# An attention and expert kernel: the router's early pass at another place, and another opening

## The chip, the cores and the metric

One of the eight cores of a Trainium2 chip runs the kernel. The metric is the device time of one execution in microseconds; several executions are timed, and the median is taken. The engines have two names each in what follows: TensorE is PE (its weight loads PEld), VectorE DVE, ScalarE ACT, GpSimd POOL, SyncE SP.

## The reference

Attention over 8 batches of 12 heads, 448 positions, 64 numbers per head; then its output is the input of an expert layer with 8 experts.

```python
q_n, k_n = rmsnorm(q, g_q), rmsnorm(k, g_k)          # x / sqrt(mean(x*x) + 1e-6) * g
scores = q_n @ k_n.T / 8;  attn = softmax(scores);  x = attn @ v
logits = x @ w_gate                                   # 3584 tokens, 8 experts
# all (token, expert) pairs in order of falling logit: a token goes to the first expert
# that still has fewer than 448 tokens
out[tokens of e] = relu(x[tokens of e] @ w1[e]) @ w2[e]
```

## The kernel before

The 96 heads are worked on in 24 groups of four (two pairs of heads). A group's q and k are loaded as rows (three quarters of each head's positions on 128 partitions, 192 numbers each, by `_load`; the last 64 positions of each head, the tails, by `_tail` or `_tails`), squared on ScalarE (L308), summed on VectorE (L320), turned into an inverse root by a logarithm and an exponential on ScalarE (L326, L328) and a correction (L337 to L339), scaled (L353, L381), split into two f16 parts (L386, L391, L420, L425), transposed, and used in three kinds of products on TensorE: a first pass that only finds row maxima (`max_scores`, L539 and L542; VectorE takes the maxima, L553), the scores (L572; ScalarE's exponential, L583), and the products with v (L607), whose results VectorE divides and ScalarE and VectorE split into two f16 parts (`x_norm` L642 to L646, `x_hi` L657 and L658, `x_lo` L663 and L664). The transposed scores come out with the keys on the partitions, so nothing is transposed there. Each pair of heads takes one bank of PSUM for its products with v, out of a ring of two banks called po. Every finished pair's x is transposed on TensorE in part (`x_here`, L681) into the same bank before the bank is given on.

Groups 0 and 1 are worked on in halves, one per pair of heads, so that TensorE gets work early. Until then dummy matmuls with the identity (`busy`, L216) keep it active; `BUSY` has their numbers. `spread` puts the product of the two norm scales g_q and g_k on all partitions by a matmul with a row of ones (L206); `spread_out` copies it to gg, by which GpSimd multiplies q (L381).

After attention comes the router. It finds for each token its best expert and an integer key, and compares the keys with thresholds; then it searches counts. `early` (L1296) does this first step for the 21 of 28 columns of tokens that belong to batches 0 to 5, as soon as their logits are there: 12 VectorE instructions (L1253 to L1263 and the compare of 128x672, L1293). The same step for the last 7 columns follows at the end of attention (the late pass). Then the experts run.

The order of all this is written out by hand, as a table: `plan` adds each step as a task with its engine or queue, what it needs and what it makes, and the table `ORDER` names the tasks two characters at a time in the order in which they are issued, so each engine's instructions stand in that order in its own line. "Yr" is the task of `early`. A step may stand anywhere in the table behind what it needs. Loads go to the queue of SyncE ("S") or ScalarE ("A"); a load that is the ninth, tenth and so on waits until the load eight before it has landed, as its semaphore is used again.

## Time and profile before

| what | |
|---|---|
| median of 3 runs | 909.04 us (906.68 to 910.67) |
| the profiled execution, its own time | 905.66 us |
| its span, first to last instruction | 903.9 us |
| TensorE busy | 860.5 us (95%) |
| VectorE, ScalarE, GpSimd busy | 642.7, 467.7, 390.4 us |
| mean granted TensorE clock | 0.982 |

Times in the profile count from the start of the span. Busy shares are averages over the whole; what a change at one place is worth is read from the rows of that place. In a timeline a row is one instruction or a run of equal ones; "[4.56 <-DVE xm L664]" says that the engine was idle for 4.56 us before it, and what ended that. A queue's rows (SPq, ACTq) are the issues of loads, not their landing. PEclk is the granted clock of TensorE as a share of 2.4 GHz; 0.5 is 1.2 GHz.

### The profile page before, as it was taken

What the parts mean: (1) busy time and instruction counts of PE and PEld (TensorE: products, weight loads), DVE (VectorE), ACT (ScalarE), POOL (GpSimd) and SP (SyncE); (2) the same over time, 40 slices, a digit from 0 to 9 for tenths busy, and PEclk for the clock granted to TensorE, in tenths of its full rate; (3) what the DMA queues carried; (4) which work ended last, traced back from release to release, by engine and by line L of the source; (5) the groups of instructions that cost most, each with busy time, mean ns of one, the idle gap of its engine ahead of it and who ended that gap; (6) DMA issues with size and microseconds to landing.
All of it is one profiled execution on the core that took longest, in us unless ns stands there. A gap on an engine that the chain in (4) does not pass through costs nothing.

```text
span 903.9 us, 27548 instructions
## 1 busy us (share of the span) xinstructions
PE 860.5 (95%) x11763; PEld 558.4 (62%) x11765; DVE 642.7 (71%) x1539; ACT 467.7 (52%) x739; POOL 390.4 (43%) x400
## 2 busy tenths in 40 slices
PE   5999999999999997995999999999999999999996
PEld 2467677777777776784556555565555655556553
DVE  6999999889988988737887776866768675143100
ACT  5987887788777874650434333323333333242110
POOL 7899998889989886001103021101111120200001
PEclk9999999999999998995999999999999999999998
DMA  7669998999999895413747195685929397591001
GB/s 188 154 153 204 189 206 175 230 186 226 161 211 199 202 171 135 90 28 137 269 146 255 38 293 171 206 231 164 253 92 279 140 251 219 170 244 43 27 18 44
DMA packets 253019, 153.64 MB, mean 170 GB/s; under 512 B 178654, under 2 KB 240094, under 8 KB 251872
## 3 DMA queue, kind: packets, MB, share of 16 engines
q1 hardware_dynamic: 247388, 129.39, 60.8%
q0 software_dynamic: 4704, 22.03, 7.4%
q8 instruction: 92, 1.51, 0.7%
q10 hardware_dynamic: 804, 0.46, 0.2%
q14 instruction: 31, 0.25, 0.1%
HBM read 94.43 MB, written 22.02 MB: 129 GB/s over the span
## 4 chain that ended last, share of the span: by engine, by line
PE 59%; issue 18%; DVE 11%; DMA 4%; POOL 3%; ACT 3%; SPq 1%; POOLq 0%; DVEq 0%; ACTq 0%
PE ph L1807 15%; PE py L1824 13%; PE po L607 12%; PE psc L572 10%; DVE mx L553 3%; PE py L1833 2%; PE pm L542 2%; DMA q<-qs 1%; DMA qkraw<-in_q_dram 1%; ACT e L583 1%; POOL out_dram L1843 1%; PE psc L542 1%; POOL rows L1740 1%; PE rp L1453 1%; DVE st L337 1%
## 5 line engine op out<-in xcount | busy, mean ns | idle before, releaser
L1807 PE MATMUL ph<-xt,w1h 128*128 128x448 f16 (+2 forms) x804 | 209.4, 344 | 0.0
L607 PEld LDWEIGHTS po<-v,e 128*64 128x64 f32 (+1 forms) x5376 | 173.5, 137 | 41.8 <-issue 21.8
L607 PE MATMUL po<-v,e 128*64 128x65 f32 (+1 forms) x5376 | 187.4, 224 | 2.3 <-DVE xt L374 1.1
L583 ACT ACTIVATE e<-psc 128x896 f32<-128x896 f32 x168 | 151.2, 915 | 48.5 <-PE psc L572 40.9
L572 PE MATMUL psc<-q,k 128*64 128x448 f16 x1344 | 156.1, 355 | 1.3 <-DVE mx L553 0.9
L1843 POOL DMA_INDIRECT out_dram<-y,idx x32 | 34.4, 1076 | 279.9 <-ACT y L1826 245.6
L1807 PE MATMUL ph<-xt,w1l 128*128 128x448 f16 (+2 forms) x402 | 135.1, 344 | 0.0
L1824 PE MATMUL py<-w2l,hh 128*128 128x384 f16 x384 | 125.0, 326 | 0.0
L1824 PE MATMUL py<-w2h,hl 128*128 128x384 f16 x384 | 125.0, 326 | 0.0
L1824 PE MATMUL py<-w2h,hh 128*128 128x384 f16 x384 | 125.0, 326 | 0.0
L1807 PEld LDWEIGHTS <-w1h 128*128 128x128 f16 x804 | 74.0, 97 | 63.8 <-issue 2.3
L553 DVE TENSOR_REDUCE mx<-pm 128x2 f32<-128x896 f32 x96 | 104.0, 1084 | 10.4 <-PE pm L542 7.8
L1795 ACT ACTIVATE hh<-ph 128x448 f16<-128x448 f32 x64 | 34.8, 544 | 144.3 <-PE ph L1807 139.6
L1824 PEld LDWEIGHTS <-hh 128*128 128x128 f16 x768 | 73.3, 97 | 46.4
L572 PEld LDWEIGHTS <-k 128*64 128x64 f16 x1344 | 75.2, 110 | 30.1 <-issue 5.7
L1826 ACT ACTIVATE y<-py 128x384 f32<-128x384 f32 x48 | 23.6, 491 | 132.6 <-PE py L1824 104.1
L1740 POOL DMA_INDIRECT rows<-xd,idx x32 | 31.9, 997 | 130.1 <-DVE idx L1634 43.2
L1797 DVE SCALAR_TENSOR_TENSOR hl<-ph,hh 128x448 f16<-128x448 f32 x64 | 39.2, 619 | 60.4 <-ACT hh L1795 60.2
L553 DVE TENSOR_REDUCE mx<-psc 128x2 f32<-128x896 f32 (+1 forms) x74 | 77.8, 1056 | 5.2 <-PE psc L542 4.5
L1727 DVE SCALAR_TENSOR_TENSOR w2l<-stage,w2h 128x768 f16<-128x768 f32 x64 | 60.2, 951 | 22.2 <-ACT w2h L1723 22.1
L1727 DVE SCALAR_TENSOR_TENSOR w1l<-stage,w1h 128x768 f16<-128x768 f32 x64 | 59.4, 950 | 3.3 <-ACT w1h L1723 3.3
L1723 ACT ACTIVATE w1h<-stage 128x1536 f16<-128x1536 f32 x32 | 47.2, 1476 | 21.5 <-DMA stage<-in_moe_w_dram 21.5
(294 smaller groups left out, 1434.3 us busy)
## 6 DMA issues: line engine op xcount, KB each, us to landing
stage<-in_moe_w_dram SPq DMA_DIRECT2D x64, 768.0 KB
vraw<-in_v_dram SPq DMA_DIRECT2D x24, 384.0 KB
xd<-xb SPq DMA_DIRECT2D x8, 1152.0 KB
qkraw<-in_q_dram SPq DMA_DIRECT2D x23, 384.0 KB
qkraw<-in_k_dram SPq DMA_DIRECT2D x23, 384.0 KB
vraw<-in_v_dram SPq DMA_DIRECT2D x24, 64.0 KB
xd<-xm SPq DMA_DIRECT2D x16, 96.0 KB
qkraw<-in_k_dram SPq DMA_DIRECT2D x22, 64.0 KB
```

The lines of the kernel that those rows point to most:

```text
L553: self.nc.vector.tensor_reduce(m, p[:, :k, :448], axis=AX.X, op=OP.max)
L572: nc.tensor.matmul(p[64 * h:64 * h + 64, i, :448], kt[:, a, n + 64 * h:n + 64 * h + 64], qt[:, a, 448 * s:448 * s + 448], start=st, stop=n ...
L583: self.nc.scalar.activation(e, p[:, :, :448], AF.Exp, scale=scale)
L607: self.nc.tensor.matmul(self.po(pair)[64 * n:64 * n + 64, w], self.T["e", d][r, i, q:q + 64], self.v1[g % 2][r, self.slot(a, u, s)], start ...
L1723: self.nc.scalar.activation(h, v, AF.Copy, scale=self.WS)
L1727: self.later(0.93, lambda w=w: self.nc.vector.scalar_tensor_tensor(l[:, w], v[:, w], self.WS, h[:, w], op0=OP.mult, op1=OP.subtract), k, i)
L1740: nc.gpsimd.indirect_dma_start(out=g[:n, c, :], out_offset=None, in_=self.xd, in_offset=bass.IndirectOffsetOnAxis(ap=idx[:n, c:c + 1], axi ...
L1795: nc.scalar.activation(hh, whole, AF.Relu)
L1797: self.later(0.6, lambda: nc.vector.scalar_tensor_tensor(hl, whole, 0.0, hh, op0=OP.max, op1=OP.subtract), k, 3.5, f)
L1807: nc.tensor.matmul(p, a[:, i, c], x[:, b, o], start=j == 0, stop=j == 17)
L1824: nc.tensor.matmul(p, a[:, f, s], b[:, f, o], start=st, stop=sp)
L1843: st = nc.gpsimd.indirect_dma_start(out=self.out, out_offset=bass.IndirectOffsetOnAxis(ap=self.router.idx[k][:n, c:c + 1], axis=0), in_=y[ ...
```

## The change

1. The task of `early` stands later in the table: behind the x_lo of pair 44 and ahead of the z of pair 45, of 48 pairs.
2. Group 0's tails are loaded by `_tails` in the form that the other groups have: one load for 64 partitions and both pairs of heads, instead of one for 128 partitions and one pair. Each half of group 0 now needs both tails of q and both of k.
3. Group 0's loads stand in another order, and the second half of k is issued by SyncE instead of ScalarE (`FQ`).
4. g_k is loaded from ScalarE's queue instead of GpSimd's, the scales' product is made on GpSimd instead of VectorE, and VectorE copies gg later.
5. The integers from which the identity is made (jp) come first on GpSimd, ahead of the clearing of buffers; some of that clearing (q2) comes later.
6. Three dummy matmuls stand ahead of the scales' matmul and 13 behind it, instead of 20 behind it.

```diff
--- before.py
+++ after.py
@@ -137,9 +137,13 @@
         self.v1 = tiles(2, [128, 16, 65], F32, "v1")

         def gain_loads():
-            for n, src in enumerate((g_q, g_k)):
-                nc.gpsimd.dma_start(self.g1[:, n], bass.AP(tensor=src.tensor, offset=src.offset, ap=[[64, 1], [1, 64]]))
+            gain_load(nc.gpsimd, 0, g_q)
             nc.gpsimd.memset(self.one, 1.0)
+
+        def gain_load(eng, n, src):
+            eng.dma_start(self.g1[:, n], bass.AP(tensor=src.tensor, offset=src.offset, ap=[[64, 1], [1, 64]]))
+
+        self.gain_load_k = lambda: gain_load(nc.scalar, 1, g_k)

         def gate_loads():
             nc.sync.dma_start(wg32[:, 0], w_gate.rearrange("(i p) e -> p i e", p=128))
@@ -172,7 +176,7 @@
                 G.memset(r[h, 4 * s + 3::8], 0.0)

         def gains():
-            nc.vector.tensor_tensor(self.g1[:, 0], self.g1[:, 0], self.g1[:, 1], op=OP.mult)
+            nc.gpsimd.tensor_tensor(self.g1[:, 0], self.g1[:, 0], self.g1[:, 1], op=OP.mult)

         wf, wo = wg32.rearrange("p a i e -> p (a i) e"), self.wg.rearrange("p a i e -> p (a i) e")

@@ -202,9 +206,11 @@

     def spread(self):

-        p = self.T["gg"] = self.bank()[:, :64]
+        p, b = self.bank()[:, :64], self.bank()
+        self.T["gg"] = p
+        self.busy(b, "early")
         self.nc.tensor.matmul(p, self.one, self.g1[:, 0], start=True, stop=True)
-        self.busy(self.bank(), "first")
+        self.busy(b, "first")

     def spread_out(self):
         self.nc.vector.tensor_copy(self.gg, self.T.pop("gg"))
@@ -216,7 +222,7 @@
             self.nc.tensor.matmul(p.rearrange("p (n c) -> p n c", c=128), idn, idn[:, None, :].to_broadcast([128, 4, 128]),
                                   start=True, stop=True)

-    BUSY = {("first",): 20, ("max", 0): 2, ("turn", 0, "q", 1): 2, ("turn", 0, "k", 1): 3, ("rows", 0, 0): 8, ("scores", 0): 2,
+    BUSY = {("early",): 3, ("first",): 13, ("max", 0): 2, ("turn", 0, "q", 1): 2, ("turn", 0, "k", 1): 3, ("rows", 0, 0): 8, ("scores", 0): 2,
             ("max", 6): 2, ("rows", 0, 1): 4, ("scores", 3): 2}

     def halves(self, g):
@@ -250,13 +256,6 @@
                       bass.AP(tensor=src.tensor, offset=src.offset + (4 * g + n - 1) * SD + 384 * self.D,
                               ap=[[64, 64], [2 * SD, 2 * groups], [1, 64]]))

-    def _tail(self, eng, src, dst, g, pair):
-
-        SD = self.S * self.D
-        eng.dma_start(dst[:, 8 * pair + 3],
-                      bass.AP(tensor=src.tensor, offset=src.offset + (4 * g + 2 * pair) * SD + 384 * self.D,
-                              ap=[[SD, 2], [64, 64], [1, 64]]))
-
     def units(self, t, a=None):

         u = t.rearrange("p (a u) d -> p a u d", a=2)[:, :, :7]
@@ -267,13 +266,15 @@
             t = self.T["raws", g // 2] = self.w.tile([128, 2, 2, 16, 64], F32, name="qkraw")
             self.T["raw", g], self.T["raw", g + 1] = t[:, :, 0], t[:, :, 1]
         i, r = divmod(n, 4 if g == 0 else 3)
-        eng = self.dma_queue("SA"[i] if g == 0 else self.load_queue(g, n))
+        eng = self.dma_queue(self.FQ[n] if g == 0 else self.load_queue(g, n))
         src = (self.q, self.k)[i]
         raw = self.T["raw", g][:, i]
         if g == 0 and r % 2:
-            self._tail(eng, src, raw, g, r // 2)
+            self._tails(eng, src, raw[:, None], g, 1 + r // 2, groups=1)
         elif g == 0:
             self._load(eng, src, raw, g, slice(r // 2, r // 2 + 1))
+            if n == 4:
+                self.gain_load_k()
         elif r:
             self._tails(eng, src, raw[:, None] if g == 1 else self.T["raws", g // 2][:, i], g, r, groups=2 - (g == 1))
         else:
@@ -286,6 +287,7 @@
         return self.LQ[n] if g > 1 else "S"


+    FQ = "SSSSAASA"
     LQ = "SSSSSS"
     VQ = "SSS"

@@ -825,7 +827,7 @@

         gain_loads, gains, gate_loads, gate_zeros, gate_high, gate_weights = self.parts
         add(-1e6 - 1, "P", 2.0, gain_loads, make="gg32", move=(1.3, 0.2))
-        add(-1e6, "D", 0.15, gains, after=["gg32"], make="gp")
+        add(-1e6, "P", 0.2, gains, after=["gg32"], make="gp")
         add(-1e6, "T", 0.3, self.spread, after=["gp", ("rc", 1)], make="gb", holds=[("po", "gg"), ("po", "busy")], frees=["busy"])
         add(-1e6, "D", 0.17, self.spread_out, after=["gb"], make="gg", frees=["gg"])
         add(P["lwg"], "S", 3.2, gate_loads, make="wg32", move=(3.2, 0.5))
@@ -847,8 +849,8 @@
             if g == 0:
                 for n in range(8):
                     i, r = divmod(n, 4)
-                    add(-1e6 + n, "SA"[i], US["load" + "SA"[i]], self.load_qk, 0, n, opens=[("raw", 0)],
-                        make=("raw", 0, i, r // 2), move=(0.63, 0.16 if r % 2 else 0.62))
+                    add(-1e6 + n, self.FQ[n], US["load" + self.FQ[n]], self.load_qk, 0, n, opens=[("raw", 0)],
+                        make=("rawt", 0, i) if r % 2 else ("raw", 0, i, r // 2), move=(0.63, 0.16 if r % 2 else 0.62))
             for n in (0, 3) if g % 2 and g > 1 else range(6) if g else ():
                 i, r = divmod(n, 3)
                 q = self.load_queue(g, n)
@@ -1029,7 +1031,7 @@
             plan.add(at, queue, us, f, *args, port=port and queue == "D", opens=() if a else opens, uses=[*uses, *opens], **kw)

         small, copy, d = US["small"], 0.58, 0.6
-        raw = [[("raw", 0, i, a) if g == 0 else ("raw", g, i)] for i in range(2)]
+        raw = [[("raw", 0, i, a), ("rawt", 0, i)] if g == 0 else [("raw", g, i)] for i in range(2)]
         e = lambda name: self.engine(name, g, a)
         us = lambda name: {"D": d, "P": 0.95}[e(name)]
         part(e("gain"), us("gain"), self.gain, *x, after=[*raw[0], "gg"], make=("qg", *x), opens=[("qn", g)], uses=[("raw", g // 2)])
@@ -1063,8 +1065,8 @@
                  port=False, frees=[("rf", *x)])

     ORDER = (
-        "0z11020+120o0-13011008071u0600051t090A030p0q14161v0r04151w1U0B181x171T191y1V1A2n1B1W1C2r1D1E2p1X1F2o1Y1G1Z1K"
+        "0z110+121014020o090A00010-131u1t1v1w1x1y2n2r2p2o0w2q2s0x0y3G3F0s040B08070p060q160r17151T18191U1V1A1B1W1C1D1E"
...
@@ -1099,10 +1101,10 @@
...
-        "WxGcXMX0XNBOX1XOLSCAGdXPX2LTX3XQLUX4CRBjXRLWX5LVXSCTYrBkQVBNQWQaBlCSQXBmQZQbQYCBLYWwLXRyCVLaXTXUCULZXVQdQcXW"
+        "LuXqLwY2LvGyLxS0GzR3R2CdQxCeR7Y6CfR8Y7CgY8LyL+LzXoR5Y9R4M0L-YAR6M1S1RBYFYGM2YHREYIM4M3YJYrR9ChRDM6M5RFS2M7M8"
...
     )
```

On VectorE, around the 12 instructions of `early`, before (st, sq and so on are names of tiles; z is that of pair 39):

```order
L374 COPY xt<-po 128x2x128
L1253 TENSOR_REDUCE best<-logits 128x21
L1254 TENSOR_TENSOR score<-logits,best 128x8x21
...
L1263 TENSOR_SCALAR key<-keyi 128x21
L1293 TENSOR_TENSOR cmp<-key,hit_80 128x672
L642 TENSOR_SCALAR z<-po 128x7
L644 RECIPROCAL z<-z 128x7
L646 TENSOR_TENSOR po<-po,z 128x7x64
```

And now, where z is that of pair 45 (the line numbers are two higher than before):

```order
L665 TENSOR_TENSOR xb<-po,xb 128x2x3x64
L666 TENSOR_TENSOR xm<-po,xm 128x64
L1255 TENSOR_REDUCE best<-logits 128x21
L1256 TENSOR_TENSOR score<-logits,best 128x8x21
...
L1265 TENSOR_SCALAR key<-keyi 128x21
L1295 TENSOR_TENSOR cmp<-key,hit_80 128x672
L644 TENSOR_SCALAR z<-po 128x7
L646 RECIPROCAL z<-z 128x7
L648 TENSOR_TENSOR po<-po,z 128x7x64
```

46 instructions of VectorE have moved ahead of the pass.

On ScalarE at the program's start, with what each waits for (sq_133 is q's, sq_134 k's; DMAHW1 is the first tail of q in both), before:

```order
L242 DMA qkraw<-in_k_dram 128x2x192
L256 DMA qkraw<-in_k_dram 128x1x64
L242 DMA qkraw<-in_k_dram 128x2x192
L256 DMA qkraw<-in_k_dram 128x1x64 [waits DMAHW1_49]
L308 ACTIVATE sq_133<-qkraw 128x7x64 [waits DMAHW0_49]
L308 ACTIVATE sq_133<-qkraw 128x7x64 [waits DMAHW4_49,DMAHW2_49]
L308 ACTIVATE sq_134<-qkraw 128x7x64 [waits DMAHW5_49,DMAHW3_49]
```

And now:

```order
L248 DMA qkraw<-in_k_dram 128x2x192
L144 DMA g_120<-in_g_k_dram 1x64
L255 DMA qkraw<-in_k_dram 64x2x64
L255 DMA qkraw<-in_k_dram 64x2x64 [waits DMAHW1_49]
L310 ACTIVATE sq_133<-qkraw 128x7x64 [waits DMAHW2_49,DMAHW0_49]
L310 ACTIVATE sq_134<-qkraw 128x7x64 [waits DMAHW7_49,DMAHW3_49,DMAHW1_49]
L310 ACTIVATE sq_133<-qkraw 128x7x64 [waits DMAHW4_49]
```

The second half of k is gone from this queue, g_k's load is in it, and k's square stands ahead of the second square of q.

## Rows read from the trace of the kernel before

**Rows 1.** Stretches: us, busy us (instructions) by engine, clock, DMA share, GB/s.

```profile
core 0: us, PE busy (x) PEld busy (x) DVE busy (x) ACT busy (x) POOL busy (x), PEclk, DMA share, GB/s
350.00:355.00 5.00, 0.93 (x8) 0.44 (x8) 3.21 (x6) 2.31 (x5) 0.90 (x1) 0.76 0.48 92
355.00:360.00 5.00, 5.00 (x72) 3.30 (x73) 2.52 (x4) 1.66 (x2) 4.06 (x4) 0.56 0.23 45
390.00:400.00 10.00, 9.91 (x283) 8.74 (x272) 3.38 (x10) 5.36 (x9) 0.00 (x0) 1.00 0.01 3
400.00:410.00 10.00, 7.73 (x224) 7.12 (x221) 5.51 (x24) 4.76 (x15) 2.64 (x9) 0.86 0.54 180
```

**Rows 2.** Timeline of TensorE: start, us, engine, line, shapes, [idle before].

```profile
345.78 0.70 PE L607 MATMUL po<-v,e 64*64 64x65 f32 x28
...
354.07 0.42 PE L681 MATMUL po<-ident,xb 128*64 128x128 f16 x4 [4.56 <-DVE xm L664]
...
355.99 1.71 PE L572 MATMUL psc<-q,k 128*64 128x448 f16 x8
...
360.27 0.95 PE L572 MATMUL psc<-q,k 128*64 128x448 f16 x8
...
396.38 3.77 PE L607 MATMUL po<-v,e 64*64 64x65 f32 x126
```

**Rows 3.** Chain of waits in order of time, 341.5 to 343: start, us, what.

```profile
341.91 0.34 DVE best L1253
```

**Rows 4.** Timeline of VectorE, 341 to 394.5.

```profile
343.27 1.61 DVE L1258 TENSOR_SCALAR keyi<-best 128x21 int32<-128x21 int32 x1
...
347.01 2.07 DVE L1262 CAST key<-keyi 128x21 f32<-128x21 int32 x1
...
349.12 2.50 DVE L1293 TENSOR_TENSOR cmp<-key,hit 128x672 bf16<-128x672 f32 x1
...
351.54 0.15 DVE L642 TENSOR_SCALAR z<-po 128x7 f32<-128x7 f32 x1
...
353.80 0.21 DVE L664 TENSOR_TENSOR xm<-po,xm 128x64 f16<-128x64 f32 x1
...
387.83 0.21 DVE L664 TENSOR_TENSOR xm<-po,xm 128x64 f16<-128x64 f32 x1
...
393.75 0.17 DVE L642 TENSOR_SCALAR z<-po 128x7 f32<-128x7 f32 x1 [5.70 <-PE po L607]
```

**Rows 5.** Timeline of ScalarE and its queue, 0 to 11.5.

```profile
7.32 0.53 ACTq L256 DMA_DIRECT2D qkraw<-in_k_dram  x1
...
7.91 0.58 ACT L308 ACTIVATE sq<-qkraw 128x448 f32<-128x448 f32 x1 [5.88 <-DMA qkraw<-in_q_dram]
...
9.02 1.04 ACT L308 ACTIVATE sq<-qkraw 128x448 f32<-128x448 f32 x2 [0.53 <-DMA qkraw<-in_q_dram]
...
10.91 0.22 ACT L326 ACTIVATE st<-st 128x14 f32<-128x14 f32 x1 [0.85 <-DVE st L320]
```

**Rows 6.** Timeline of all engines, 0 to 16: SyncE's queue, TensorE.

```profile
0.75 0.46 SPq L242 DMA_DIRECT2D qkraw<-in_q_dram  x1
...
1.27 0.73 SPq L256 DMA_DIRECT2D qkraw<-in_q_dram  x1
...
5.31 0.59 SPq L242 DMA_DIRECT2D qkraw<-in_q_dram  x1
...
8.12 6.04 PE L216 MATMUL po<-ident 128*128 128x512 f16 x20
```

**Rows 7.** Timeline of GpSimd, 343 to 349.

```profile
343.06 1.79 POOL L353 TENSOR_TENSOR kn<-qkraw,st 128x896 f32<-128x896 f32 x1
...
346.91 2.14 POOL L381 TENSOR_TENSOR qn<-qn,gg 128x896 f32<-128x896 f32 x1
```

**Rows 8.** Timeline of VectorE, 407 to 411: the late pass.

```profile
408.96 0.17 DVE L1262 CAST key<-keyi 128x7 f32<-128x7 int32 x1
...
409.28 0.38 DVE L1293 TENSOR_TENSOR cmp<-key,hit 128x224 bf16<-128x224 f32 x1
```

**Rows 9.** DMA issues, 0 to 16: out<-in, queue, KB, us to landing.

```profile
g<-in_g_q_dram POOLq DMA_DIRECT2D x1, 0.2 KB, 3.2
```

More of the change, by code (lines that the diff above doesn't have):

```diff
@@ L1065 @@
     ORDER = (
-        "0z11020+120o0-13011008071u0600051t090A030p0q14161v0r04151w1U0B181x171T191y1V1A2n1B1W1C2r1D1E2p1X1F2o1Y1G1Z1K"
-        "0w1a2q1L1c2s1H0x1b1M1J0y1N1+3GCi1i1-3F2M1j1I200sCj2O1z1k21Ck2N2LCm221dCo2P231O1l1e242Q1mCp252t1fCl261hCn272R"
+        "0z110+121014020o090A00010-131u1t1v1w1x1y2n2r2p2o0w2q2s0x0y3G3F0s040B08070p060q160r17151T18191U1V1A1B1W1C1D1E"
+        "031X1F1Y1G1Z1K1a1L1c1H1b1M1J1N1+Ci1i1-2M1j1I20Cj2O1z1k21Ck2N2LCm221dCo2P231O1l1e242Q1mCp252t1fCl26051hCn272R"
         "1g1P282v2u1Q2SCq1R1S2T292C2w1r2U3hG+Cr3m2V2DH0G-3k0C2A2W492xH1Cs3jCt2y2aCu3iCw2B2b2E1sCxH23HCv3l2z4A2G2X2k2Y"
@@ L1101 @@
         "LILHCOBMQIC3C5XDGTXEGULJRxAvQUW-C4XFXGLKGVQOLLXHGWQRW+XIC6GYLMGXQSLNLOBiXJCPC9QQLPGZGaQPC7XKLQXLCQAwGbC8QTLR"
-        "WxGcXMX0XNBOX1XOLSCAGdXPX2LTX3XQLUX4CRBjXRLWX5LVXSCTYrBkQVBNQWQaBlCSQXBmQZQbQYCBLYWwLXRyCVLaXTXUCULZXVQdQcXW"
-        "LcLbXXQfCWLdQgXYGeCXGfQiLeCYCZGgQeQhLfXZGhRzGjCCCaLgGiQmLhLiXaXbXcGkBoLjCbGlQlWyQjXdLkBnGmGnQkBpGoQnLlLmXeCD"
-        "QoCcCEQpCFXfLnCGGpXgGqR+QtXhGrQwBqGsCIQqXiXjQvLoGuXkQrLpQuXlLqGtXpQsLrXyLsXzXrR-LtGvX+CHR1GxR0QzQ-X-Y0Q+QyGw"
-        "Y1LuXqLwY2LvGyLxS0GzR3R2CdQxCeR7Y6CfR8Y7CgY8LyL+LzXoR5Y9R4M0L-YAR6M1S1RBYFYGM2YHREYIM4M3YJR9ChRDM6M5RFS2M7M8"
+        "WxGcXMX0XNBOX1XOLSCAGdXPX2LTX3XQLUX4CRBjXRLWX5LVXSCTBkQVBNQWQaBlCSQXBmQZQbQYCBLYWwLXRyCVLaXTXUCULZXVQdQcXWLc"
+        "LbXXQfCWLdQgXYGeCXGfQiLeCYCZGgQeQhLfXZGhRzGjCCCaLgGiQmLhLiXaXbXcGkBoLjCbGlQlWyQjXdLkBnGmGnQkBpGoQnLlLmXeCDQo"
+        "CcCEQpCFXfLnCGGpXgGqR+QtXhGrQwBqGsCIQqXiXjQvLoGuXkQrLpQuXlLqGtXpQsLrXyLsXzXrR-LtGvX+CHR1GxR0QzQ-X-Y0Q+QyGwY1"
+        "LuXqLwY2LvGyLxS0GzR3R2CdQxCeR7Y6CfR8Y7CgY8LyL+LzXoR5Y9R4M0L-YAR6M1S1RBYFYGM2YHREYIM4M3YJYrR9ChRDM6M5RFS2M7M8"
         "RIM9MARJRHRARCRMMBYNRGYOYPRLMCYQRKYRMDY3S3RTYWYXRSYYRPYZRORNY4YaRQRRYKYeYfYbYgYLYSYcYhYBYUYiXsYDYTYlY5YdYCYn"
```

## The prediction, made before the changed kernel was run

> **What bounds the kernel now.** I read the busy shares first: TensorE is the only engine near its span, so a microsecond counts where TensorE stands still or runs slowly. The stretches of the trace show one such place in the attention part. From 350 to 355 us TensorE is busy 0.93 of 5.00 us, and the granted clock averages 0.76 there and 0.56 from 355 to 360; around it, from 390 to 400, TensorE is busy nearly throughout at 1.00 [rows 1]. The timeline of TensorE shows the stall itself: four small transposes at 354.07 stood behind 4.56 us of idle time, ended by VectorE's last part of an x (L664) [rows 2]. The chain of waits passes through the early pass: its first instruction, at 341.91, is a piece of the chain [rows 3]. VectorE's timeline shows the rest: the pass runs from 341.91 to 349.12 + 2.50 = 351.62, 9.71 us, and only then z of the pair whose transposes TensorE waits for, at 351.54, up to that pair's xm, which ends at 353.80 + 0.21 = 354.01 [rows 3, 4]. So VectorE's line, and in it a step that nobody needs before the router, makes the stall.
>
> The second place is the opening, where there is no cover. ScalarE's first square (7.91) stands behind 5.88 us of idle time, ended by a load of q; right before it ScalarE's own queue issued a tail of k, at 7.32, which waits until the first tail of q has landed [rows 5]. That tail of q was issued at 1.27 [rows 6]; it took 7.32 - 1.27 = 6.05 us.
>
> **The early pass moved.** It leaves 341.91 and comes 46 VectorE instructions later, behind the xm that starts at 387.83 and ahead of the z at 393.75.
>
> At the old place: the z needs the 28 products that end at 345.78 + 0.70 = 346.48 [rows 2]. From z to the end of xm the trace takes 354.01 - 351.54 = 2.47 us [rows 4], so the transposes can go at 346.48 + 2.47 = 348.95. TensorE comes to them at 354.07 - 4.56 = 349.51 [rows 2], 0.56 us later: the wait goes altogether, 4.56 us. The clock is at half for (1 - 0.76) x 5 / 0.5 = 2.4 us of the first stretch and (1 - 0.56) x 5 / 0.5 = 4.4 us of the second [rows 1], so from about 352.6 to 359.4, 3.1 us after TensorE went idle. TensorE worked from 354.07 to 359.4 in it, 5.3 us. The same eight score matmuls take 1.71 us there and 0.95 us just behind it [rows 2], so of the 5.3 us some 5.3 x (1 - 0.95/1.71) = 2.4 us, at most half, 2.7 us, come back: I take 2.5. Sum here **-7.1 us** (-4.6 if something else keeps the clock low, -7.3 at best). Late next would be the exponentials that feed the products; in the same pattern from 390 to 400 they cost TensorE nothing [rows 1].
>
> At the new place: between xm (ends 388.04) and the z at 393.75 VectorE idles 5.70 us, waiting for TensorE [rows 4]. Does the pass fit? At the old place it is stretched by GpSimd: its 1.61 us TENSOR_SCALAR ends at 344.88, when GpSimd's kn has ended at 344.85; its 2.07 us CAST ends at 349.08, when GpSimd's qn has ended at 349.05 [rows 4, 7]. At the new place GpSimd does nothing (0.00 from 390 to 400) [rows 1]. The late pass does the same steps on 7 columns instead of 21: 0.17 us for the CAST, 0.38 for the compare [rows 8]. At three times these, 0.51 and 1.14, and 0.51 for the TENSOR_SCALAR too, the pass shrinks by 1.56, 1.36 and 1.10 us to at most 9.71 - 4.02 = 5.69 us, and some of the other nine steps were stretched too. So it just fits or fits well: **0**. The other end is no shrinking at all: 9.71 - 5.70 = 4.0 us late, straight onto TensorE, because the last pair of heads needs the bank that this z's pair holds. I take 0, as the row of the CAST is that of the same instruction.
>
> **The opening.** A tail is now 64 partitions with both pairs of heads in one load, so the first square needs two tails of q, and the first square of k two tails of k. On ScalarE's queue the second tail of k still waits for the first tail of q. What a load of the new form takes no row shows. From below: the gain's small load landed 3.2 us after its issue [rows 9]. From above: the first half of q, six times a tail's bytes, was issued at 0.75 and had landed when the next load that waits for it went out at 5.31 [rows 6], 4.6 us; or as slow as the old tail, 6.05 us. At 3.2 us the first tail of q is there at 1.27 + 3.2 = 4.5, the second tail of k at 7.7; k's first square (0.58 us, the row of the first square) ends at 8.3, q's second at 8.8, and the first logarithm goes at about 8.9 instead of 10.91 [rows 5]: -2.0 us. At 4.6 us k's first square ends at 1.27 + 2 x 4.6 + 0.6 = 11.0 against 9.02 + 1.04 = 10.06 [rows 5], +0.9 us. I take **-2.0**: a tail has a sixth of the half's bytes, so its size is not what made the old one slower than the half load, and the new one has 64 outermost entries where the old one had 2. The Trainium skill speaks both ways here. "DMA: Bandwidth & Descriptors", in its section on why a DMA increments its semaphore by 16, says that a load is spread over as many of the 16 DMA engines as divide its outermost sizes, which is 2 for the old tail and 16 for the new one; no row shows single engines. The rules for kernel authors of the same page say not to split a transfer into two partition halves, since they share the same engines and serialize; by that rule this term is 0 and the sum -7.1. What follows the first logarithm are the same instructions with the same waits until TensorE is full, so I carry the 2.0 us through.
>
> At nothing I cost these. The norm scales' product on GpSimd and their load on ScalarE's queue are hidden by the wait for the first root, since the scaled q is not needed before; uncovered it would be the 3.2 us of a load [rows 9]. The memsets of q2 now stand between GpSimd's first normalisations, where it waits for VectorE's root. VectorE's gg copy is now behind memsets that it had to do anyway. SyncE issues one load more ahead of group 1's, 0.73 us at the longest [rows 6], hidden because ScalarE squares group 0 first. TensorE's dummies, which ended at 14.16 with the first transposes behind them, are 16 instead of 20, at 6.04/20 = 0.30 us each [rows 6]. If the scale product goes at about 5, the 13 behind it end near 9.5, and the transposes come near 12: idle for some 2.5 us, less than the 3.1 us after which the clock fell in the one stall.
>
> **Sum:** -7.1 + 0 - 2.0 = -9.1 us. The profiled execution is at 905.66 and would come to 896.6. It lies 3.4 us under the median of the runs, 909.04; against the median the forecast is **899.9 us**.
>
> **The rivals.**
> A. The opening gives nothing: the tails' halves serialize, or the second tail of k, which goes out late, takes what the first won. For it: no row has the new form, and two loads hang on one another. Time 909.04 - 7.1 = 901.9, at the +0.9 end 902.8. The Trainium skill's rule on partition halves ("DMA: Bandwidth & Descriptors", rules for kernel authors) is this case. Chance 0.17.
> B. At the old place another wait follows: the exponentials or the last group's GpSimd chain hold TensorE for up to 2.5 us. Against it: VectorE and GpSimd get 9.7 us of contention less. Time 899.9 + 2.5 = 902.4. Chance 0.10.
> C. Slower: the pass does not shrink. TensorE then idles 4.0 us ahead of the last pair, longer than 3.1 us, so the clock falls: the 126 products of 3.77 us [rows 2] cost 0.8 x 3.77 = 3.0 more, and of the transposes and gate products up to where it fell anyway (0.86 mean from 400 to 410, 7.73 us busy [rows 1]) some 6 us cost 4.8 more. 4.0 + 3.0 + 4.8 = 11.8 against 9.1: 909.04 + 2.7 = 911.7. It decides from a pass of 5.70 + 3.1 = 8.8 us on. Against it: GpSimd is idle there. Chance 0.04.
> D. The pass takes 6 to 8 us: up to 2.3 us late, clock kept. 899.9 + 2.3 = 902.2, with the opening lost 904.2. Chance 0.05.
> E. The change does not do what it says: TensorE's stall at 354 is not the pass's but another wait shows under it at once, and only the opening is left: 907.0. Against it: z stands directly behind the pass. Chance 0.04.
>
> **How the numbers follow.** The forecast has 0.60. A measurement of this kernel can tell about 0.5%, 4.5 us, from no change, so faster means under 904.5. The forecast, A, B and most of D are faster: 0.60 + 0.17 + 0.10 + 0.04 = 0.91, less 0.07 for runs that scatter over 4 us: 0.84. Slower is C: 0.04. The rest is 0.12. The range reaches from 896.0 (the lowest run, 906.68, with 7.3 and the 2.0, and 1.4 for tails faster than 3.2 us) to 905.1 (D, and the opening at its +0.9 end: 902.2 + 2.9).
>
> **What would show it.** Right: no idle time over 1 us before the small transposes near 347 us, granted clock 1.00 from 340 to 400, VectorE's pass near 380 us within 6 us with the CAST under 0.6 us, its following z still waiting for TensorE, the first square near 6 us and the first logarithm near 9. Wrong: a CAST that is still long, TensorE idle before the last 126 products, a first logarithm at 10.9 or later, or a new wait of several microseconds at 347 to 355.

## The result, and the profile after

The changed kernel takes 898.34 us (median of 4 runs, 896.53 to 898.73); the kernel before, beside it, 908.72 (906.68 to 910.67). The ratio is 0.9882, with a 95% interval of 0.9856 to 0.9908: 8.4 to 13.1 us less, where 9.1 were forecast. The two profiled executions differ by less: their own times are 905.66 and 898.33 us, and their spans 903.9 and 896.6. That of before lies 3 us under its median, and that of after lost something on the way, as will be seen.

**Where the pass stood.** Stretches of the changed kernel, columns as in [rows 1]:

```profile
350.00:355.00 5.00, 5.00 (x104) 3.37 (x100) 4.61 (x8) 2.37 (x4) 4.08 (x4) 1.00 1.11 121
355.00:360.00 5.00, 5.00 (x105) 3.47 (x101) 4.21 (x7) 3.97 (x8) 3.44 (x4) 1.00 0.74 177
380.00:390.00 10.00, 9.91 (x260) 8.36 (x258) 5.38 (x21) 6.51 (x9) 0.00 (x0) 1.00 0.01 3
390.00:400.00 10.00, 9.19 (x280) 8.66 (x276) 4.81 (x15) 5.11 (x15) 0.35 (x3) 1.00 0.30 82
```

TensorE is busy all of 350 to 360 now, at 1.00. Its timeline, at the transposes that stood behind 4.56 us of idle time in [rows 2], has no bracket any more:

```profile
348.27 0.87 PE L609 MATMUL po<-v,e 128*64 128x65 f32 x24
348.97 0.28 PE L683 MATMUL po<-ident,xb 128*64 128x128 f16 x4
```

**Where the pass stands.** VectorE's timeline, old place and new one, to be held against [rows 4]:

```profile
346.14 0.17 DVE L644 TENSOR_SCALAR z<-po 128x7 f32<-128x7 f32 x1 [4.63 <-PE po L609]
...
380.42 0.32 DVE L1255 TENSOR_REDUCE best<-logits 128x21 f32<-128x168 f32 x1
...
381.15 0.17 DVE L1260 TENSOR_SCALAR keyi<-best 128x21 int32<-128x21 int32 x1
...
382.30 0.17 DVE L1264 CAST key<-keyi 128x21 f32<-128x21 int32 x1
...
382.51 0.85 DVE L1295 TENSOR_TENSOR cmp<-key,hit 128x672 bf16<-128x672 f32 x1
...
386.20 0.17 DVE L644 TENSOR_SCALAR z<-po 128x7 f32<-128x7 f32 x1 [2.84 <-PE po L609]
```

At the old place VectorE waits for TensorE now. At the new one the pass runs from 380.42 to 382.51 + 0.85 = 383.36, 2.94 us instead of 9.71, and z behind it still waits 2.84 us for TensorE.

**The opening.** ScalarE and its queue, to be held against [rows 5]:

```profile
1.31 0.56 ACTq L144 DMA_DIRECT2D g<-in_g_k_dram  x1
1.91 3.56 ACTq L255 DMA_DIRECT2D qkraw<-in_k_dram  x2
5.63 0.58 ACT L310 ACTIVATE sq<-qkraw 128x448 f32<-128x448 f32 x1 [3.60 <-DMA qkraw<-in_q_dram]
7.05 1.04 ACT L310 ACTIVATE sq<-qkraw 128x448 f32<-128x448 f32 x2 [0.84 <-DMA qkraw<-in_k_dram]
8.39 0.22 ACT L328 ACTIVATE st<-st 128x14 f32<-128x14 f32 x1 [0.30 <-DVE st L322]
```

The first square comes 2.28 us earlier, the first logarithm 10.91 - 8.39 = 2.52. TensorE has no gap ahead of its first transposes: the 13 dummies take 5.65 us, 0.43 each, from 5.73 to 11.38, and the transposes start at 11.47. All the same the granted clock is at 0.5 from 17.99 to 21.41 us in this trace (0.80 in the stretch from 15 to 20, 0.86 from 20 to 25).

**Where the opening's gain went in this trace.** Take VectorE's instructions and ScalarE's exponentials, which from 30 us on have the same order in both kernels apart from the pass, and subtract the start in the trace of before from the start in another trace. The median for those that start in ten microseconds of before is that kernel's lead there (negative: earlier, so -2.5 is a lead of 2.5 us):

```
start in before:      30     130     190     210     250     340     360     440
pass alone         +0.95   +0.90   +0.33   +0.52   +1.28   +0.72   -6.46   -5.69
opening alone      -2.48   -2.53   -2.74   -2.40   -2.20   -2.55   -2.73   -2.75
changed kernel     -2.24   -2.28   -2.69   -0.04   +0.35   -0.37   -7.55   -7.30
the same again     -2.45   -2.48   -2.45   -1.31   -0.85   -1.77   -8.95   -8.03
old tails          -2.48   -2.15   -2.24   -1.11   -0.82   -0.91   -8.09   -8.02
GpSimd busy        -2.02   -2.07   -1.77   -1.32   -1.05   -1.55   -8.73   -8.36
scale first        -0.29   -0.35   -0.53   -0.96   -0.50   +0.35   -6.82   -6.05
20 dummies         -2.61   -2.72   -2.41   -2.42   -0.38   -1.03   -8.21   -8.24
g_k on GpSimd      -2.71   -2.81   -3.09   -3.51   -3.53   -4.53  -11.70  -11.72
corrections later  -2.12   -1.87   -1.84   -2.26   -1.56   -0.89   -8.06   -6.71
k's half on SyncE  +1.14   +1.03   +0.42   +1.27   +1.25   +1.08   +0.93   +0.92
tails ahead        +0.35   +0.29   +0.06   +1.19   +1.73   +0.45   +0.40   +0.37
g_k on ScalarE     +1.48   +1.45   +2.27   +1.85   +1.86   +1.53   +1.38   +1.36
```

Each line is one execution (the kernels are those of the experiments; the last three have the pass at its old place and the old opening but for one edit). The trace of before is itself an early one: pass alone and the last three lines are 0.35 to 1.48 us behind it at 30 us already.

Between 340 and 360 every kernel with the pass moved gains 7.17 to 7.18 us; opening alone, where it stays, gains 0.18. Between 360 and 440 four of the nine executions with the pass moved (pass alone, the same again, scale first, corrections later) give 0.77 to 0.93 us of it back near 405: there the granted clock falls 2.0 to 2.8 us before the last gate products end. In the other five it falls between 0.3 us before that end and 0.8 behind it, and in the five with the pass at its old place always 0.07 to 0.25 us behind it. What decides this no run shows.

The changed kernel, though, has lost its opening's 2.5 us before it gets there, most of it near 200 us. VectorE, GpSimd and TensorE there:

```profile
198.07 1.74 DVE L339 TENSOR_TENSOR st<-st 128x28 f32<-128x28 f32 x1
199.84 0.19 DVE L340 TENSOR_TENSOR st<-st 128x28 f32<-128x28 f32 x1
...
200.17 0.62 DVE L648 TENSOR_TENSOR po<-po,z 128x448 f32<-128x448 f32 x1
```

```profile
197.88 1.89 POOL L427 TENSOR_TENSOR qs<-qn,qs 128x896 f16<-128x896 f32 x1
```

```profile
202.21 0.37 PE L683 MATMUL po<-ident,xb 128*64 128x128 f16 x4 [1.20 <-DVE xm L666]
```

```profile
200.00:205.00 5.00, 3.80 (x54) 2.57 (x52) 3.63 (x8) 4.17 (x7) 4.55 (x4) 0.73 1.10 193
```

A step of a norm's correction on 128x28 numbers, 0.19 us in the row behind it, ends at 199.81; GpSimd's instruction that began just before it ends at 199.77. The division of a finished pair stands behind it, TensorE idles 1.20 us, and the clock, 0.73 in this stretch, 1.00 before it and 0.93 behind it, takes more. In the trace of before the same step (at 200.60) took 0.77 us. It is the same collision as that of the pass, at a place the change does not touch: which of the two engines comes first there shifts by fractions of a microsecond.

### The profile page after: what moved, and what is told of

It is laid out like the page before. It is cut to its first block, busy times and chain, and to the rows that moved or that the text cites. A ratio compares the mean times of both kernels' runs of the same rounds, so it can differ in the third digit from the quotient of the medians.

```text
span 896.6 us, 27538 instructions
## 1 busy us (share of the span) xinstructions
PE 863.0 (96%) x11759; PEld 558.4 (62%) x11761; DVE 636.4 (71%) x1538; ACT 467.3 (52%) x739; POOL 390.0 (43%) x400
## 4 chain that ended last, share of the span: by engine, by line
PE 63%; issue 18%; DVE 8%; DMA 4%; POOL 4%; ACT 3%; POOLq 0%; SPq 0%; ACTq 0%; DVEq 0%
PE ph L1809 15%; PE py L1826 13%; PE po L609 12%; PE psc L574 11%; DVE mx L555 3%; PE py L1835 2%; PE pm L544 2%; DMA q<-qs 2%; POOL out_dram L1845 1%; PE psc L544 1%; ACT e L585 1%; POOL rows L1742 1%; PE rp L1455 1%; DMA qkraw<-in_k_dram 1%; DVE st L339 1%
```

## The experiments

Ratios are to the kernel before, measured on the same chip.

**1. The pass alone.** Kernel before, one task moved in the table:

```diff
-...XSCTYrBkQV...   ...M3YJR9Ch...
+...XSCTBkQV...     ...M3YJYrR9Ch...
```

> The kernel before with the early pass moved alone (behind the x_lo of pair 44), opening as before. My theory: the pass was the whole of TensorE's stall at 349.5 to 354.1 us and of the half clock behind it, and at the new place it shrinks because GpSimd is idle: -7.1 us against the kernel before (about 901.6), the pass within 3.5 us at the new place, its CAST under 0.3 us, no idle time of TensorE over 1 us between 345 and 360. Rival 1: the new place depends on the other phase that the opening gives; the pass alone gives only the stall without the clock, -4.6 us, or a wait of up to 2.5 us shows at the old place. Rival 2: nothing of the gain is the pass's: 0 to -2 us, and the opening made the rest.

Measured: 0.9925 (0.9910 to 0.9941), 5.3 to 8.2 us less. In the trace no idle time of TensorE over 0.5 us is left between 345 and 360, and the lead grows by 7.18 us. The pass takes 2.95 us there, its CAST 0.17. The first theory holds; both rivals are out.

**2. The opening alone.** The changed kernel, the pass at its old place (the same move, backwards).

> The changed kernel with the early pass back at its old place, so that the opening is all that differs from the kernel before. In the trace of the changed kernel everything up to 190 us is 2.2 to 3.0 us earlier than before, and from 205 us only 0.04 us: VectorE's first step of the norm's correction (L339) took 1.74 us there under GpSimd's work, TensorE idled 1.20 us and its clock stood at half for 3.4 us. My theory: the opening is worth 2.5 us, and what happens near 200 us is a matter of one execution: the median is 2.5 us under the kernel before, the first logarithm at 8.4. Rival: the new opening shifts GpSimd and VectorE against one another near 200 us in every execution, so the 2.5 us are always given back there: 0 within 0.7 us, first logarithm at 8.4 all the same. Under both the stall near 350 us stands as before, 4 to 5 us.

Measured: 0.9987 (0.9972 to 1.0002), 12 runs from 902.20 to 908.51 us: between 2.5 us less and 0.2 more; by the medians, 904.09 and 906.06, 2.0 less. TensorE's stall is where it was:

```profile
351.51 0.42 PE L683 MATMUL po<-ident,xb 128*64 128x128 f16 x4 [4.56 <-DVE xm L666]
```

In this execution, one of 902.79 us, the lead lasts (the step near 198 us took 1.10); the slowest two, at 908.16 and 908.51, cannot have kept it. Neither theory is right as it stands: some 2.5 us at the start, of which a part, different each time, reaches the end.

**3. The changed kernel again**, beside 1, 2 and 4.

> The changed kernel itself, beside the three others on the same chip, so that they can be compared with it: 0.9882 of the kernel before, about 10 us less. If the loss near 200 us is one execution's, its trace shows another shift there this time; if it is built in, L339's first step near 198 us takes about 1.7 us again and TensorE idles about 1.2 us near 202.

Measured: 0.9897 (0.9881 to 0.9913). The step near 198 us took 1.74 us again, TensorE idled 1.20 at 202; the lead fell from 2.45 to 1.31, by less than in the first trace, since the clock stayed up. So the stretch recurs, and what it costs varies. On this chip the two parts alone make 6.8 and 1.2 us, together 8.0; the whole makes 9.3 (7.9 to 10.8). So the opening is worth more on top of the moved pass than alone: 2.5 us by the medians (899.49 and 897.01), against 1.2 to 2.0.

**4. The old form of the tails.**

```diff
-            self._tails(eng, src, raw[:, None], g, 1 + r // 2, groups=1)
+            self._tail(eng, src, raw, g, r // 2)
... (and `_tail` as before; each half needs its own pair's tail alone again)
```

> The changed kernel with the tails of group 0 in the old form (one load for 128 partitions and one pair of heads), all else as in the changed kernel: order, queues, early pass. Theory 1, the form did it: the first square waits for q's first tail as before, at about 7.9 us instead of 5.6, the first logarithm comes at 10.4 to 10.9 instead of 8.4, 2.0 to 2.5 us more than the changed kernel. Theory 2, order and queues did it (loads on two queues, the second half of k on SyncE's): the first logarithm stays within 0.5 us of 8.4 and the time is that of the changed kernel.

Measured: 0.9888 (0.9872 to 0.9903), like the changed kernel. ScalarE's timeline:

```profile
5.55 0.58 ACT L317 ACTIVATE sq<-qkraw 128x448 f32<-128x448 f32 x1 [3.52 <-DMA qkraw<-in_q_dram]
...
8.28 0.20 ACT L335 ACTIVATE st<-st 128x14 f32<-128x14 f32 x1
```

The form of the tails, on which the prediction had put the opening's gain, is not needed for it.

**5 and 6. The queue, or the order, of the loads.** Kernel before; in 5 the second half of k is issued by SyncE, in 6 both second tails stand ahead of the second halves.

```diff
5:
-        eng = self.dma_queue("SA"[i] if g == 0 else self.load_queue(g, n))
+        eng = self.dma_queue(("S" if n == 6 else "SA"[i]) if g == 0 else self.load_queue(g, n))
6, in the table:
-0+120o0-13011008
+0+120o1014010-08   (and 13 where 14 stood)
```

> The kernel before with one edit of the opening: the second half of group 0's k is issued by SyncE instead of ScalarE, behind the second half of q. The old form of the tails reached the first square at 5.55 us in the run with old tails, against 7.91 and 7.49 in the kernel before: the form is not the cause. Theory 1, the queue is: two loads of 192 KB out of two queues at once hold up the first tail of q; now the first square comes at 5.5 to 6.5 and the first logarithm 1.5 us or more earlier than 10.9. Theory 2, the order is: the second half of q right behind the first tail is enough to hold it up: first square still at 7.0 to 7.9, first logarithm within 0.4 us of 10.9.

> The kernel before with another single edit of the opening: on both queues the second tail stands ahead of the second half (ScalarE then issues the second half of k only when the first tail of q has landed). Theory 2, the order is the cause: first square at 5.5 to 6.0, first logarithm near 8.5 to 9.2, about 2 us less time. Theory 1, the queue is the cause: much the same here, because the second half of k goes out late as well; but then the run with the second half of k on SyncE shows it too. If neither run moves the first logarithm, it is a third thing (the norm scales' loads, the identity's order on GpSimd).

Measured: 0.9997 (0.9983 to 1.0011) and 0.9995 (0.9983 to 1.0008). First squares at 7.25 and 7.64, first logarithms at 12.05 and 11.27, later than before. Neither the queue nor the order does it by itself.

**7. g_k's load between k's half and k's tail.** Kernel before with g_k loaded from ScalarE's queue (`gain_loads` loads g_q alone):

```diff
+            if n == 4:
+                self.gain_load_k()
```

> The kernel before with only g_k's load moved from GpSimd's queue to ScalarE's, behind the first half of k and so ahead of the first tail of k, which goes out at about 1.9 us instead of 1.3 (the second half of k then waits for the first tail of q, as it did in the run with the tails ahead, which gained nothing). Neither the form of the tails, nor the queue of k's second half, nor the order of tails and halves brought the first square from 7.2 to 7.9 us down to 5.6. Theory 3: the first tails of q and of k, issued at 1.27 and 1.30 on two queues, hold each other up, and the 0.6 us that g_k's load puts between them let q's tail through: first square at 5.3 to 6.0. Rival: g_k's load on GpSimd's queue made no difference and it needs two of the edits together: first square at 7.0 or later.

Measured: 0.9986 (0.9970 to 1.0002). ScalarE and its queue, then VectorE:

```profile
4.94 0.43 ACTq L246 DMA_DIRECT2D qkraw<-in_k_dram  x1
...
5.80 0.54 ACTq L260 DMA_DIRECT2D qkraw<-in_k_dram  x1
6.39 0.58 ACT L314 ACTIVATE sq<-qkraw 128x448 f32<-128x448 f32 x1 [4.36 <-DMA qkraw<-in_q_dram]
...
10.38 0.22 ACT L332 ACTIVATE st<-st 128x14 f32<-128x14 f32 x1 [1.20 <-DVE st L326]
```

```profile
6.26 0.57 DVE L1152 TENSOR_SCALAR ident<-jp 128x128 f16<-128x128 int32 x1 [4.35 <-POOL jp L1152]
...
8.98 0.29 DVE L1152 TENSOR_SCALAR before<-jp 128x128 bf16<-128x128 int32 x1
9.20 1.68 DVE L326 TENSOR_REDUCE st<-sq 128x7 f32<-128x455 f32 x3
```

The load at 4.94 waits for q's first tail, as the one at 7.32 in [rows 5] did, the one at 6.91 in the run with the pass alone and the one at 7.21 in 6. So q's first tail lands 2 us earlier once k's goes out 0.6 us later, as theory 3 has it. The packets in the traces show the two tails one behind the other (a tail is 128 packets of 256 bytes): in the kernel before, the first 128 of ScalarE's queue start from 3.71 to 4.80 us, those of SyncE's from 4.46 to 6.12; here SyncE's start from 3.31 to 4.35, and those of k's tail from 4.49 on. The first square, at 6.39, misses theory 3's 5.3 to 6.0 for another reason: the load at 5.80, which waits for q's second half, stands ahead of it on ScalarE.

The first logarithm gains only 0.5 us: the first square is done, but VectorE makes the identity at 6.26, waiting for GpSimd's integers, and comes to the first sum at 9.20. By these rows the opening's gain takes two edits: q's tail early, and the integers early (VectorE makes the identity at 2.54 us in the changed kernel). No run has these two alone, and the time can't tell: 0.9986 here, 0.9987 with the whole opening (run 2). This trace is 1.48 us behind that of before at 30 us, with the clock at 0.50 from 20 to 25.

**8. The changed kernel with g_k back on GpSimd's queue.**

```diff
             gain_load(nc.gpsimd, 0, g_q)
+            gain_load(nc.gpsimd, 1, g_k)
...
-            if n == 4:
-                self.gain_load_k()
```

> The changed kernel with g_k's load back on GpSimd's queue. The tails of k then go out at 1.3 and 1.9 us on ScalarE's queue, and the second no longer waits for the first tail of q (which it did because g_k's load made it the ninth). Theory 3 (the two first tails hold each other up, g_k's load between them is what helps): first square at 7 us or later again, the time 2 us over the changed kernel. Theory 1 of the run with old tails (the new form does not collide): first square at 5.0 to 5.8, and with k's second tail out 3 us earlier the first logarithm at 7.4 to 8.2 instead of 8.4; in the time 0 to 0.7 us less than the changed kernel, as g_k then lands at about 6 us and the scaled q comes later.

Measured: 0.9904 (0.9888 to 0.9920), as the changed kernel; first square at 5.52, first logarithm at 7.59. With the new form the first tails do not hold each other up, wherever g_k's load stands: their packets start side by side, from 3.25 to 3.82 and from 3.56 to 3.99 us. So the form does matter, as one of two ways out: the old form with g_k's load between (4), or the new form. The first logarithm, 0.8 us earlier again, shows in the lead (2.71 at 30 us) but not in the time. (The lead grows to 4.53 by 340 in this execution, the fastest of the six at 893.91; the median is 896.89.)

**9. GpSimd busy beside the pass at its new place.**

```diff
-        for f in self.bests(0, self.EARLY):
+        for i, f in enumerate(self.bests(0, self.EARLY)):
             f()
+            if i == 0:
+                for n in range(10):
+                    G, x = self.nc.gpsimd, self.B[:, 0:1, None].to_broadcast([128, 7, 64])
+                    G.tensor_tensor(self.load, self.load if n else x, x, op=OP.add)
... (and the tile `load`)
```

> The changed kernel, with ten additions of 128x448 f32 put on GpSimd beside the early pass at its new place; they are released by the pass's first instruction, and nothing reads what they make. In the traces of the changed kernel the pass takes 2.94 us there (380.42 to 383.36), at the old place 9.7. Theory 1: GpSimd's work is what stretches VectorE: with some 0.95 us for each addition the single conversions and integer steps (0.16 to 0.18 us in the changed kernel) wait for the addition in hand, and the pass takes 5 to 10 us; beyond 5.8 us TensorE waits for z before the last pair, up to 4 us more in the time. Theory 2: the old place was slow for another reason (the transfers there, or ScalarE at PSUM): the pass stays at 2.9 to 3.3 us and the time is that of the changed kernel, 0.989 of the kernel before.

Measured: 0.9911 (0.9887 to 0.9935). VectorE, then GpSimd:

```profile
379.97 0.86 DVE L1261 TENSOR_SCALAR keyi<-best 128x21 int32<-128x21 int32 x1
380.75 0.25 DVE L1258 TENSOR_TENSOR score<-score,rankt 128x168 bf16<-128x168 bf16 x1
380.91 0.94 DVE L1262 TENSOR_TENSOR keyi<-best,keyi 128x21 int32<-128x21 int32 x1
...
383.78 0.16 DVE L1265 CAST key<-keyi 128x21 f32<-128x21 int32 x1
...
383.99 1.60 DVE L1296 TENSOR_TENSOR cmp<-key,hit 128x672 bf16<-128x672 f32 x1
385.51 0.15 DVE L644 TENSOR_SCALAR z<-po 128x7 f32<-128x7 f32 x1
```

```profile
380.88 9.56 POOL L1305 TENSOR_TENSOR load<-load,best 128x448 f32<-128x448 f32 x9
```

The pass takes 379.24 to 385.59, 6.35 us: steps of 0.17 us take 0.73 to 0.94, about one addition of GpSimd. z stands directly behind it, and the lead falls by 0.47 us (8.73 to 8.26 by 400 us): over the gap by little, late by little. In the time it does not show beside the 0.9897 of run 3. This is theory 1, and it is the decision point of the prediction's term, met from the other side.

**10. More dummies.** The changed kernel:

```diff
-    BUSY = {("early",): 3, ("first",): 13,
+    BUSY = {("early",): 3, ("first",): 17,
```

> The changed kernel with 17 dummies behind the scales' matmul instead of 13, so 20 in all as before. In four traces of the changed opening TensorE idled 0.56 (opening alone and others 0.6), 1.27 and 2.03 us between the dummies and the first transposes; in the runs with 1.27 and 2.03 its clock stood at half from 13.5 to 16.9 and from 13.0 to 23.3 us, and of the opening's 2.5 us 2.0 and 0.3 were left at 30 us. Theory: four dummies more (1.2 us) close that gap: clock at full throughout 11 to 30 us, but where the loads are early they hold the transposes back by 0.6 us, so the time is within 1 us of the changed kernel and its runs scatter less. Rival: the clock falls all the same (the idle time at 17 us, 1.02 us, is enough): a half-clock stretch before 30 us in this trace too.

Measured: 0.9904 (0.9887 to 0.9922), the same as the changed kernel. The transposes stand directly behind the dummies, the lead at 30 us is 2.61, and the clock stays at 1.00 to 30 us. Whether the dummies did that, one trace can't say, and the gap ahead of the transposes does not decide it: the clock stayed at 1.00 to 30 us in opening alone, where TensorE idled 1.61 us there (the expectation above has 0.56 to 0.6), and in old tails with 1.13; it fell in GpSimd busy with 1.27, and in the changed kernel's own trace with 0.09. What a long stretch at half clock goes with there is seen in run 11, whose TensorE had

```profile
5.32 5.09 PE L222 MATMUL po<-ident 128*128 128x512 f16 x13
12.44 0.56 PE L451 MATMUL po<-ident,ks 128*128 128x128 f16 x7 [2.03 <-DVE ks L422]
```

and in stretches (PE, PEld, VectorE, ScalarE, GpSimd, clock, as in [rows 1])

```profile
10.00:15.00 5.00, 2.50 (x18) 1.27 (x16) 3.70 (x12) 3.69 (x9) 4.22 (x5) 0.80 1.07 276
15.00:20.00 5.00, 4.93 (x18) 1.60 (x17) 4.91 (x11) 3.43 (x9) 4.35 (x5) 0.50 1.04 208
20.00:25.00 5.00, 5.00 (x27) 2.39 (x26) 4.36 (x7) 4.11 (x8) 3.75 (x5) 0.67 0.00 0
```

k's square came at 8.02 there (2.15 us of waiting for k's load), the transposes late, and of the opening's lead 0.29 us were left. Of the 1.95 us lost against the changed kernel 0.97 is the later first logarithm (9.36 against 8.39); the rest comes behind it, where the clock is at half.

**11. The division ahead of the correction near 200 us.** The changed kernel, in the table:

```diff
-...8PJR82Us...
+...JR82Us8P...
```

> The changed kernel with two neighbouring steps of VectorE's line exchanged near 200 us: the division of pair 20's products goes ahead of the three small steps of group 14's correction (L339 to L341), which GpSimd's work stretched to 1.74 us in two traces of the changed kernel, with TensorE idle 1.20 us behind it. Theory: that stretch is what takes the opening's gain back: TensorE's idle time before pair 20's small transposes goes to under 0.3 us, and the time falls by 1.2 us, by up to 2.9 where the clock had fallen, against the changed kernel (0.9897 of before on this chip). Rival: GpSimd's next normalisation waits for the correction and comes 0.6 us later, and group 14's transposes bring the wait back later: same time as the changed kernel, within 0.5 us.

Measured: 0.9885 (0.9868 to 0.9903), not to be told from the changed kernel. The wait at 202 is gone in the trace (the lead grows there, from 0.53 to 0.96), but by 340 us nothing is left of it.

**12. The corrections later at three places**, on top of 8.

```diff
-...8PJR82Us...   ...6-...Tz...   ...9j...Vf...
+...JR82Us8P...   ...Tz6-...      ...Vf9j...
```

> The kernel with g_k on GpSimd's queue, and at three places of VectorE's line the three small steps of a norm's correction (L339 to L341 of the changed kernel) go one step later: behind the division of pair 20 near 200 us, and behind the copies of pairs 13 and 25 (L376) near 150 and 242 us. In the traces so far TensorE waited there for VectorE, whose correction stood still until GpSimd's instruction ended: 0.44 to 1.27 us near 150, 0.2 to 1.2 near 202, 0.6 to 2.3 near 242, and from 140 to 345 us the kernels with the new opening lost between 0 and 2.5 us of their lead over the trace of the kernel before. Theory: these three waits go under 0.3 us, the lead at 345 us is that at 140 us or more, and the time is 1 to 2 us under the 0.990 that the changed kernel and its variants have, at 0.988 to 0.989 of the kernel before. Rival: GpSimd's normalisations, which need the correction, move the waits behind them: waits of the same size near 155, 205 or 250 us, and no gain in the time.

Measured: 0.9928 (0.9915 to 0.9942), against 0.9904 (0.9888 to 0.9920) of its base, run 8, measured on another chip: no gain, and whether it is slower the two intervals, which overlap, leave open. The three waits for VectorE are under 0.33 us, and another has come:

```profile
229.81 0.76 PE L573 MATMUL psc<-q,k 128*64 128x448 f16 x6 [1.55 <-DMA q<-mt]
```

a row of maxima that comes by DMA is late. My theory fell: the three waits went and the time did not. That a step taken from one wait is found in the next fits this row, but is not shown for each wait. No version beat the changed kernel by more than the runs scatter.

## Why the prediction was right, point by point

- **The pass leaves its old place, -7.1 us:** right, -7.18 in each trace between 340 and 360, and 5.3 to 8.2 in the time. The lead grows by 5.0 us up to the stretch from 350 and by 2.2 behind it, near the 4.6 of idle time and 2.5 of clock in the sum.
- **The new place costs 0:** right at the pass, and for the reason given. GpSimd is idle and the pass shrinks to 2.94 us, far under the bound of 5.69: six of its twelve steps had been stretched, not three, and the compare takes 0.85 us, less than three times the late pass's 0.38. What the prediction did not have is the clock's earlier fall near 405 us, which takes 0.77 to 0.93 us in four of the nine executions with the pass moved. Run 9 put the stretch back. The Trainium skill, "SBUF — State Buffer", section "SBUF: two separate sides", says that VectorE and GpSimd share one pair of ports, and that of a GpSimd instruction and a VectorE instruction in a two-port mode or with two inputs in SBUF whichever starts first keeps the pair for the whole instruction; the ends at 199.81 and 199.77 agree.
- **The opening, -2.0 us:** 2.52 at the first logarithm, but the cause was wrong, "the new one has 64 outermost entries where the old one had 2": run 4 has 8.28 with the old form. q's first tail was slow because k's in the same form went out beside it and went first (packets, run 7), and VectorE's late identity would have hidden most of the gain (run 7). The Trainium skill, "DMA: Bandwidth & Descriptors", section on why a DMA increments its semaphore by 16, has the old form on the two lowest-numbered engines, which would put both tails on the same two; runs 7 and 8 agree, though no row shows single engines. The Trainium skill's rule against partition halves (the same page, rules for kernel authors) would have the form give nothing: run 4 fits that (8.28 with the old form, 8.39 with the new), run 8 does not, where the new form alone keeps the first tails apart.
- **"I carry the 2.0 us through":** wrong as a reason, though not shown wrong in size. The same instructions do not have the same waits in each execution. Of seven executions with the changed opening (the lines opening alone to 20 dummies) the lead at 340 us over the trace of before is 1.12 us on average, from 2.55 ahead to 0.35 behind. Four traces with the old opening (before, pass alone, k's half on SyncE, tails ahead) are 0.56 behind the trace of before on average there. Held against these, the changed opening is 2.7 us ahead at 30 us and 1.7 at 340. TensorE is busy up to there, yet it waits at places where VectorE's small corrections meet GpSimd, and whether they meet changes with each shift; in some executions the clock falls in the opening besides. In the time 1.2 us are left (0 not excluded) with the pass at its old place, and 2.5 with the pass moved. So the 2.0 came near because more was won at the start than forecast and part of it was lost: that is luck, not the reason given.
- **"Idle for some 2.5 us, less than the 3.1 us after which the clock fell":** wrong twice. The gap was not there: a dummy takes 0.43 us in the changed kernel's trace and not 0.30, so the 13 end at 11.38 and not near 9.5, and the transposes follow at 11.47. And the number drawn from one stall does not hold here: the granted clock fell in the changed kernel's trace without that gap (at 17.99 us), in run 9 after 1.27 us of idle time and in run 11 after 2.03, while with 1.13 (run 4) and 1.61 us (run 2) it stayed up. What takes the clock down in the opening stays open.
- **The sum** was -9.1; the two measurements give -10.7 (-13.1 to -8.4) and -9.3 (-10.8 to -7.9). Whether its opening term is too large can't be told: 1.2 us alone, 2.5 on top of the moved pass.
- **The rivals:** B, C, D and E did not come. A's mechanism, k's second tail as the late load, shows in two executions of the same opening: in runs 9 and 11 k's square waits 1.70 and 2.15 us for k's load, and of the lead at 30 us 2.02 and 0.29 were left.

## What to carry to other kernels

A step that nobody needs soon belongs in a gap where the engine that stretched it is idle; the room it needs is its undisturbed time, a third of what its old place showed. A gain at the start of a long, tightly ordered program need not be a gain at its end: compare the same instruction's start along the traces, of more than one execution of each kernel, before the term is carried through. And before a load's shape is blamed, look at what goes out beside it on the other queue.

## What the runs showed of the hardware

- Two tail loads in the old form, issued at 1.27 and 1.31 us on two queues: the load that waits for the first goes out at 6.91 to 7.32. With the second issued at 1.90, at 4.94 (run 7) and 4.97 (run 4). The packets of the two tails run one behind the other (3.71 to 4.80 and 4.46 to 6.12 us in the kernel before), in the new form side by side (3.25 to 3.82 and 3.56 to 3.99 us, run 8).
- VectorE's step of 128x28 f32 (0.17 to 0.19 us) takes 1.74 us under one instruction of GpSimd and ends within 0.04 us of it; an integer TENSOR_SCALAR of 128x21 takes 0.86 instead of 0.17. The bf16 steps of 128x168 between them keep 0.25, but they stand where one addition of GpSimd has ended and the next begins, so they don't show that their form is spared.
- The idle time ahead of the first transposes does not order the executions by clock: it stayed at 1.00 to 30 us with 0.54 (run 8), 0.60 (run 3), 1.13 (run 4) and 1.61 us (run 2), and fell to 0.5 with 0.09 (the changed kernel), 1.27 (run 9) and 2.03 (run 11).
- Behind attention the granted clock fell 0.07 to 0.25 us after the last gate product in the five executions with the stall near 350 us, and 2.0 to 2.8 us before it in four of the nine without.
